# Attention and a mixture of adapters on one core: the stores of a tile, the queue of transposes and the order table

## The chip, the cores and the metric

The kernel runs on one core of a Trainium2 chip. The metric is the device time of one execution in microseconds. The kernel before took 182.09 us (median of three runs, 181.49 to 182.18).

The core's engines each work through their own list of instructions, in order: TensorE (PE; its weight loads are PEld), VectorE (DVE), ScalarE (ACT), GpSimd (POOL) and SyncE (SP). SP does nothing but issue transfers. Transfers run on 16 DMA engines, whichever engine issued them.

## The reference

```python
scores = scale * np.matmul(q, k.transpose(0, 1, 3, 2))     # 8 batches, 12 heads, 448 rows, 64 wide
attn = np.maximum(scores, 0.0) ** 2 / S
attn_out = np.matmul(attn, v)
x = attn_out.transpose(0, 2, 1, 3).reshape(3584, 768)
logits = x @ w_gate                                        # 8 experts
# the two best experts of a row, weighted by a softmax over the two
delta[row] += w[row, e] * (x[row] @ A[e]) @ B[e]           # A: 768x16, B: 16x768
return x + delta                                           # 3584 x 768, float32
```

The attention uses a squared ReLU in place of a softmax, so no row has to be normalised. The adapters are low-rank: 16 columns per expert, and the eight experts side by side make 128.

## The kernel before, in words

**Attention.** Twelve heads are four by four: three groups `q` of four heads, called quads, for each of the eight batches `b`. A quad goes through seven steps `j` of 64 key rows, each step with all 448 query rows, which makes 21 steps per batch and 174 steps `n` in all (the last 128 query columns of batch 7 are a part of their own, with several `j` in one step). The words of a step are `qk n` (scores, TensorE, into two PSUM banks), `relu n` (ACT or DVE, PSUM to SBUF in bf16), `sq n` (DVE, squares two or three steps at once) and `pv n` (TensorE, accumulates over the seven steps). `x m` copies the finished quad into `k.xt`, the transposed output of the attention (ACT or DVE). `tp` and `te` transpose the q and k of the next quad on TensorE and copy them out on DVE. The loads of q, k and v are cast to bf16 on the way and are issued from POOL, two transfers for each tensor of a quad (`load`, L185). Their words are `f` and a number: `f14` is k of quad 2, `f15` v of quad 0, `f16` q of quad 3, `f17` k of quad 3, `f22` the two instructions that make the selection matrix `sel`.

**Adapters.** The 3584 output rows are 28 tiles `t` of 128 rows, two blocks `j` of 64 rows each. For a group of three tiles `z` projects on all experts and the gate, the words `gmax` to `gzp` choose and weigh two experts, `zt` and `zT` transpose the weighted projection. Then for each tile and each half `h` of its 768 columns, `b 2t+h` multiplies with `B` (L714) and adds x by three matmuls with an identity (L705); `o 2t+h` copies the result from PSUM to the buffer `osb` (L743), and `st 2t` stores the tile (L760). For tiles 15 to 23 x doesn't come from matmuls: SP transposes `k.xt` back by DMA, six transposes for a group of three tiles (`turned`, words `xb`, L655), and `o` adds them on DVE (L734).

**The order.** The whole program is written in the order of the table `ORDER`: 1113 words, from which each engine gets its own list. `:A` or `:D` names the engine of a copy, `@` the first PSUM bank. A search made the table offline, with a cost for each word that stands in `build` as `op(engine, microseconds, ..., lat=...)`; these costs do nothing in the kernel. An engine waits where its next instruction waits, with all that stands behind it.

**Buffers.** `POOLS` gives the number of each: four of `osb`, eight of v, five each of q and k, three of `xb`. A buffer is free again when the last instruction that uses it is done; for `osb` that is when the store has landed. A tile that needs a buffer takes one whose store stands earlier in the table.

**Stores.** `st` (L752) walks the 128 rows of a tile in runs of 64, one transfer each. The output is seen as `out.rearrange("(b p j) f -> b j p f", b=8, j=7)`: a block `j` is 64 rows `p` that lie seven output rows apart, each 768 floats (3,072 bytes) long. The stores of tiles 24 and 26 are issued from ACT, those of the others from SP; tile 27 is stored in two halves of its columns, one from SP and one from ACT. The search gave a store 1.4 us of its queue and a landing 1.9 us later, and made each `xb` wait for the store of the tile six before its group (`xlag`).

Of the kernel before, what the change touches and what calls it, by code (L numbers as in the profile page):

```python
# [14 lines left out]
J = 7  # L15
# [14 lines left out]
PARTS = {b: ((0, S, 1),) for b in range(NB)}  # L30
PARTS.update({7: ((0, 320, 1), (320, 448, 4))})


C = dict(late=6, xi=(), om=(), merge_x=0, sqs=(2, 2, 3), xback=(15, 23), xblat=1.4, xbdur=1.35, bx=8, xlag=6, xh=2, apart=3, apcap=1, gl=(3, 1), tqlat=2.0)
GROUP = 2688
POOLS = dict(qT=5, a=11, zp=2, zT=3, osb=4, w=3, q=5, k=5, v=8, xb=3)
# [3 lines left out]
f4 f3 f1 f0 f2 f6 f5 f8 f7 f11 f9 f10 f84@0 f12 f88 f85@2 f90 f89 f13 f87@4 qk0@6 f91 qk1@0 qk2@2 relu0:D qk3@4  # L40
f14 relu1:A relu2:D relu3:A tp2@6 f17 qk4@0 relu4:A te2 qk5@4 qk6@2 sq2 relu5:A tp3@6 f16 f86@0 relu6:A te3 sq0
qk7@0 f15 qk8@4 qk9@6 relu7:A tp4@2 relu8:D relu9:A f18 qk10@0 te4 qk11@4 relu10:A qk12@6 sq4 tp5@2 relu11:A f19
qk13@0 relu12:A te5 tp6@4 f26 relu13:A sq9 qk14@2 qk15@6 tp7 relu14:A f23 sq7 pv0@0 pv1 pv2 relu15:A pv3 qk16@2
te6 pv4 pv5 relu16:A f20 pv6 qk17@6 x13:D pv7@4 relu17:A qk18@2 sq11 pv8 f22 pv9 x12:A qk19@6 relu18:A pv10
qk20@0 relu19:D f21 pv11 relu20:A pv12 pv13 qk21@2 x27:A sq16 qk22@6 f27 qk23@0 relu21:A aw1@5 sq14 relu22:A f33
relu23:A x26:D qk24@2 tp8@6 ae1 f25 relu24:A qk25@0 sq18 qk26@4 tp9 relu25:A f55 pv14@2 pv15 pv16 relu26:A pv17
te8 qk27@0 pv18 f31 pv19 relu27:A pv20 sq23 qk28@4 qk29@6 x41:A f28 qk30@0 relu28:A x40:D aw0@3 sq25 relu29:A
f29 relu30:A qk31@4 tp10@6 ae0 tp11 relu31:A f32 sq21 qk32@0 qk33@2 relu32:A te10 pv21@4 pv22 f30 relu33:A pv23
qk34@0 sq30 qk35@6 relu34:A qk36@2 f37 relu35:D relu36:A qk37@0 pv24 pv25 pv26 relu37:A sq32 qk38@2 f35 tp12@6
pv27 relu38:A tp13 qk39@0 x55:A te12 f43 qk40@2 x54:A z0@5 relu39:A sq35 qk41@6 f34 z1 relu40:A qk42@0 relu41:D  # L50
z2 relu42:A qk43@2 f38 gmax0 relu43:A tp14@6 sq28 qk44@0 tp15 relu44:A f42 qk45@2 gd0 gu0 te14 relu45:A qk46@0
gt0 relu46:A f50 sq39 qk47@6 pv28@2 pv29 pv30 gsg0 pv31 relu47:A qk48@0 f24 pv32 pv33 gw0 sq44 pv34 relu48:A f48
qk49@6 x69:A gzp0 tp18@0 relu49:A tp19 sq37 f36 pv35@4 zt0@3 zt1 zt2 x68:A qk50@6 te18 zT0:A pv36 f41 pv37
relu50:A qk51@2 pv38 sq46 pv39 relu51:A pv40 qk52@0 f47 qk53@6 pv41 relu52:A tp16@2 x82:D tp17 relu53:A te16
qk54@0 b2@4 relu54:A sq49 f44 qk55@6 o2:A qk56@2 qk57@0 relu55:A relu56:D b0@4 f49 x83:A relu57:D qk58@6 o0:A
qk59@2 relu58:A z3@5 z4 f39 sq51 relu59:A qk60@0 qk61@6 z5 sq56 relu60:A b4@4 f40 relu61:A gmax3 qk62@2 sq58
b1@0 relu62:A f46 gu3 gd3 o4:A qk63@6 gt3 sq42 qk64@2 gsg3 o1:A b3@1 f65 relu63:A gw3 b5@4 gzp3 relu64:A sq60
f51 zt3@0 zt4 zt5 o3:A pv42@6 pv43 o5:A qk65@2 st2 pv44 zT3:A pv45 sq53 qk66@4 relu65:A pv46 pv47 pv48 tp20@0
relu66:A st4 qk67@2 tp21 x96:D x97:A f53 te20 pv49@4 relu67:A pv50 qk68@6 st0 pv51 pv52 relu68:A pv53 sq63 f66
pv54 pv55 qk69@0 qk70@2 x110:A relu69:D qk71@6 f45 relu70:A b6@4 relu71:A x111:D qk72@0 o6:D tp22@2 relu72:A  # L60
sq65 qk73@6 tp23 pv56@4 pv57 relu73:A f74 qk74@0 te22 pv58 pv59 relu74:A pv60 qk75@6 f79 pv61 sq67 pv62 relu75:A
qk76@2 b8@0 relu76:A x124:D qk77@6 f64 x125:A sq70 tp24@2 relu77:A tp25 qk78@4 z6@1 te24 f59 relu78:A qk79@6 z7
relu79:A o8:D qk80@4 qk81@2 f52 sq72 z8 relu80:A b10@0 relu81:A gmax6 sq77 f54 qk82@6 tp26@4 o10:A tp27 qk83@2
relu82:A gd6 gu6 b7@0 te26 f56 relu83:A qk84@6 gt6 o7:D qk85@4 gsg6 relu84:A qk86@2 gw6 f70 sq74 b9@0 relu85:A
pv63@6 pv64 relu86:A gzp6 pv65 qk87@4 pv66 sq79 pv67 relu87:A pv68 pv69 zt6@1 zt7 x139:A x138:D zt8 qk88@2 o9:A
qk89@4 zT6:D qk90@6 relu88:A st8 relu89:D tp28@0 tp29 relu90:A qk91@2 f80 te28 pv70@4 pv71 relu91:A pv72 pv73
qk92@6 f60 sq84 pv74 pv75 relu92:A pv76 qk93@0 b14@2 x153:D x152:A f58 relu93:A sq81 qk94@6 tp30@4 o14:A tp31
pv77@0 relu94:A pv78 f77 qk95@2 te30 pv79 pv80 relu95:A pv81 qk96@6 pv82 f57 sq91 pv83 relu96:A qk97@4 b11@2
relu97:D x166:A f67 b12@3 x167:A o11:A sq93 qk98@6 o12:A st10 qk99@0 qk100@4 relu98:A relu99:D b13@2 relu100:A
z9@3 st6 sq88 qk101@6 o13:A tp32@0 qk102@4 relu101:A tp33 b15@2 st12 f62 sq86 relu102:A qk103@6 o15:A te32 f61  # L70
qk104@4 relu103:A z10 z11 sq100 relu104:A qk105@0 f69 pv84@6 pv85 pv86 relu105:A gmax9 qk106@4 pv87 sq95 f72
pv88 relu106:A pv89 pv90 qk107@0 x181:A qk108@4 f63 gd9 gu9 x180:A relu107:D b16@2 relu108:A gt9 qk109@6 o16:D
f81 pv91@0 gsg9 pv92 relu109:A gw9 pv93 sq105 qk110@4 pv94 pv95 relu110:A pv96 f78 qk111@6 gzp9 pv97 relu111:A
x195:D zt9@2 zt10 qk112@4 sq98 x194:A zt11 f75 b17@3 relu112:A zT9:D qk113@6 o17:A sq102 pv98@0 qk114@4
relu113:A pv99 st16 tp36@2 pv100 tp37 relu114:A pv101 qk115@6 te36 pv102 pv103 relu115:A st14 pv104 tp34@4 tp35
f83 sq109 qk116@2 x209:A qk117@6 x208:A b20@1 relu116:A f68 te34 b22@0 relu117:A f71 sq114 o20:A qk118@2 qk119@4
qk120@6 relu118:A b21@1 f73 sq112 o22:A b23@2 relu119:A o21:D z12@3 sq107 relu120:A st20 qk121@0 qk122@4
relu121:A z13 relu122:D z14 o23:A qk123@6 pv105@0 gmax12 pv106 relu123:A qk124@4 gd12 pv107 gu12 pv108 gt12
sq116 pv109 relu124:A pv110 pv111 qk125@6 f82 b18@2 gsg12 relu125:A gw12 x223:D x222:A qk126@4 f76 o18:D qk127@6
relu126:A b19@1 gzp12 sq121 relu127:A zt12@0 zt13 zt14 qk128@2 pv112@4 pv113 o19:D relu128:A qk129@6 pv114  # L80
zT12:D pv115 st18 pv116 relu129:A pv117 sq123 pv118 tp38@2 qk130@0 x236:A tp39 qk131@6 st22 relu130:A b24@4 te38
relu131:A tp42@0 sq119 tp43 x237:A qk132@2 b25@6 relu132:A te42 xb90 b28@7 o24:A o25:A sq128 xb93 qk133@2 o28:A
qk134@4 tp40@0 relu133:A sq126 pv119@6 tp41 pv120 relu134:A pv121 xb91 qk135@2 te40 pv122 pv123 relu135:A pv124
pv125 qk136@4 x251:D xb94 qk137@0 x250:A b29@2 sq130 relu136:A b26@3 st24 relu137:A sq135 o29:A qk138@6 qk139@4
o26:A qk140@0 xb92 z15@2 relu138:A relu139:D z16 z17 relu140:A qk141@6 st28 gmax15 pv126@4 pv127 relu141:A gd15
pv128 gu15 qk142@0 gt15 sq133 pv129 pv130 gsg15 pv131 relu142:A xb108 qk143@6 pv132 gw15 b27@3 gzp15 x264:A
x265:D relu143:A zt15@2 xb111 zt16 zt17 sq137 pv133@0 o27:A qk144@4 tp44@6 zT15:A pv134 tp45 relu144:A xb95
qk145@2 pv135 te44 pv136 relu145:A pv137 qk146@4 pv138 pv139 st26 sq140 relu146:A z18@6 b30@7 x279:A sq142 z19
x278:A xb109 qk147@2 qk148@4 qk149@0 o30 relu147:A z20 sq144 b32@7 relu148:A xb112 relu149:A b33@2 gmax18 xb110
qk150@4 o32 qk151@0 relu150:A b31@3 gu18 o33 relu151:A gd18 qk152@4 sq149 st32 b34@7 relu152:A gt18 o31 gsg18  # L90
qk153@0 qk154@4 gw18 o34 relu153:A b35@2 st30 gzp18 relu154:A qk155@0 o35 pv140@6 relu155:A pv141 sq151 qk156@4
xb113 pv142 pv143 relu156:A qk157@2 qk158@0 pv144 pv145 relu157:D relu158:A pv146 tp46@4 tp47 x293:A x292:D
qk159@0 qk160@2 relu159:A zt18@7 te46 zt19 xb126 zt20 z21@6 relu160:A z22 sq156 zT18:A qk161@0 qk162@4 qk163@2
relu161:A xb129 b40@7 sq147 relu162:A z23 sq158 relu163:A qk164@0 xb127 pv147@4 pv148 pv149 relu164:A pv150
qk165@2 o40 pv151 pv152 relu165:A pv153 sq154 qk166@0 xb130 b41@7 relu166:A gmax21 x307:A gu21 qk167@2 gd21
pv154@0 sq163 x306:A pv155 pv156 st34 relu167:A pv157 pv158 qk168@4 gt21 o41 pv159 gsg21 pv160 b36@2 gw21 x320:A
gzp21 xb128 x321:A b38@3 sq161 relu168:A zt21@7 zt22 sq165 zt23 qk169@0 st40 zT21:A pv161@4 pv162 pv163
# [47 lines left out]
def build(k=None, c=C):  # L145
# [104 lines left out]
    def aw_place(half, deps):  # L250
# [13 lines left out]
        def ev():  # L264
# [5 lines left out]


    order = [(b, u, q, range(j, min(j + PARTS[b][u][2], J))) for b in range(NB) for u in range(len(PARTS[b]))
             for q in range(QUADS) for j in range(0, J, PARTS[b][u][2])]
    NS = len(order)
    first_use, last_use = {}, {}
    head_of, heads = {}, {}
# [654 lines left out]
```

## Time and profile before

| | us |
|---|---|
| median of three runs | 182.09 |
| the profiled execution, its own time | 182.88 |
| its span, first to last instruction | 180.8 |
| PE busy | 165.2 (91%) |
| DVE busy | 163.6 (90%) |
| ACT busy | 156.4 (87%) |
| POOL busy | 89.9 (50%) |
| first store issued | 61.9 |
| last matmul begins | 175.4 |
| last store issued | 177.0 |

The busy times are those of the page's first part; a span holds idle time at both ends, about 7 us until the first step and 4.3 us after the last copy. Three engines are near 90% busy over the whole span, and all three are nearly without a gap between 24 and 160 us. "Busy" counts an instruction from its start to its modelled end; matmuls overlap, so PE's figure is an upper one. The share of a DMA queue is the time that its packets took, as a share of 16 engines' time; packets of one engine can overlap, so that slices over 1 occur.

### The profile page before, as it was taken

The numbers are of one execution on the slowest core, as the hardware profiler recorded it, in microseconds if no ns is written. First come the engines' busy times: TensorE is split into PE (matmuls) and PEld (weight loads), VectorE is DVE, ScalarE is ACT, GpSimd is POOL, SyncE is SP. The second block draws the span as 40 slices with busy tenths as digits, with TensorE's granted clock in tenths as the row PEclk, the third lists the DMA queues.
The fourth block names the chain that finished last, engine by engine and source line by source line (L and its number), as shares of the span: only waits on it lengthen the run. The fifth ranks groups of instructions, "written<-read, shape, count | busy, mean of one in ns | idle before, by whom it ended". The sixth has DMA issues, their size and how long they took to land.

```text
span 180.8 us, 7744 instructions
## 1 busy us (share of the span) xinstructions
PE 165.2 (91%) x3366; PEld 99.2 (55%) x3366; DVE 163.6 (90%) x254; ACT 156.4 (87%) x240; POOL 89.9 (50%) x155
## 2 busy tenths in 40 slices
PE   7777889788999999999999899999999999999990
PEld 2434466454555565655646475655666557676640
DVE  0799799999989999999999899999999999999740
ACT  3499899999999999999999999999999899992120
POOL 7998998979669377760877487340000000000000
PEclk9997899999999999999999999999999999999999
DMA  5999999999999999996599999997376579467875
GB/s 94 127 175 180 156 142 179 182 184 164 214 142 146 186 237 194 176 178 141 68 143 287 224 181 259 224 170 202 68 126 144 131 175 110 101 149 176 227 215 172
DMA packets 34450, 30.50 MB, mean 169 GB/s; under 512 B 11952, under 2 KB 30896, under 8 KB 34416
## 3 DMA queue, kind: packets, MB, share of 16 engines
q0 software_dynamic: 22000, 17.03, 64.9%
q1 hardware_dynamic: 11792, 11.90, 26.5%
q10 hardware_dynamic: 624, 1.08, 2.2%
q8 instruction: 26, 0.43, 1.0%
q14 instruction: 8, 0.07, 0.1%
HBM read 33.84 MB, written 11.01 MB: 248 GB/s over the span
## 4 chain that ended last, share of the span: by engine, by line
PE 51%; ACT 27%; POOL 7%; DMA 6%; issue 4%; DVE 3%; ACTq 0%; DVEq 0%; POOLq 0%
ACT a L468 24%; PE ps L714 18%; PE ps L449 11%; PE ps L516 10%; DMA q<-in_q_dram 6%; PE ps L560 4%; PE ps L310 3%; PE ps L705 3%; POOL q L185 3%; POOL k L185 3%; PE ps L622 2%; ACT osb L743 2%; DVE a L485 2%; ACT xt L544 1%; POOL k_rest L216 1%
## 5 line engine op out<-in xcount | busy, mean ns | idle before, releaser
L468 ACT ACTIVATE a<-ps 128x896 bf16<-128x896 f32 (+3 forms) x158 | 132.6, 952 | 3.7 <-PE ps L449 3.1
L485 DVE TENSOR_TENSOR a<-a 128x1792 bf16<-128x1792 bf16 (+3 forms) x75 | 89.0, 1200 | 0.0
L449 PE MATMUL ps<-qT 64*64 64x448 bf16 (+2 forms) x756 | 58.1, 342 | 3.9 <-ACT a L468 2.4
L714 PE MATMUL ps<-B,zT 128*128 128x384 f32 x112 | 47.5, 515 | 0.0
L516 PE MATMUL ps<-a,v 64*64 64x448 bf16 (+2 forms) x756 | 45.3, 335 | 1.6 <-DVE a L485 1.3
L449 PEld LDWEIGHTS <-qT 64*64 64x64 bf16 x756 | 25.1, 105 | 31.8 <-issue 23.2
L185 POOL DMA_DIRECT2D k<-in_k_dram x46 | 27.9, 629 | 18.2 <-PE ps L310 7.3
L185 POOL DMA_DIRECT2D v<-in_v_dram x48 | 29.0, 629 | 6.2 <-PE ps L449 1.8
L185 POOL DMA_DIRECT2D q<-in_q_dram x48 | 29.4, 651 | 4.9 <-DMA v<-in_v_dram 2.7
L516 PEld LDWEIGHTS <-v 64*64 64x64 bf16 x756 | 22.7, 108 | 9.0 <-issue 4.1
L324 DVE COPY qT<-ps 128x1792 bf16<-128x1792 bf16 x21 | 22.8, 1085 | 0.2
L544 ACT CAST xt<-ps 128x448 bf16<-128x448 f32 (+2 forms) x37 | 19.0, 554 | 2.9 <-PE ps L516 2.7
L743 ACT COPY osb<-ps 128x384 f32<-128x384 f32 x26 | 13.1, 523 | 7.1 <-PE ps L714 4.1
L714 PEld LDWEIGHTS ps<-B,zT 128*128 128x128 f32 x112 | 17.3, 190 | 3.3 <-issue 0.3
L470 DVE TENSOR_SCALAR a<-ps 128x896 bf16<-128x896 f32 (+1 forms) x16 | 16.9, 1067 | 0.5 <-PE ps L449 0.5
L310 PEld LDWEIGHTS <-q 64*64 64x64 bf16 x672 | 10.4, 111 | 6.3 <-issue 2.5
L560 PEld LDWEIGHTS <-xt 128*128 128x128 bf16 x168 | 10.5, 98 | 5.8 <-issue 4.7
L560 PE MATMUL ps<-awg,xt 128*128 128x136 bf16 x168 | 13.5, 223 | 0.0
L705 PEld LDWEIGHTS <-xt 128*128 128x128 bf16 x114 | 8.0, 98 | 9.9 <-issue 8.1
L310 PE MATMUL ps<-identb,q 64*64 64x64 bf16 x672 | 10.8, 196 | 2.5 <-DMA q<-in_q_dram 1.3
L705 PE MATMUL ps<-identb,xt 128*128 128x128 bf16 x114 | 12.7, 220 | 0.2
L544 DVE CAST xt<-ps 128x448 bf16<-128x448 f32 (+2 forms) x17 | 9.6, 571 | 2.2 <-PE ps L516 2.2
(47 smaller groups left out, 97.5 us busy)
## 6 DMA issues: line engine op xcount, KB each, us to landing
out_dram<-osb SPq DMA_DIRECT2D x50, 192.0 KB, 3.9
q<-in_q_dram POOLq DMA_DIRECT2D x48, 112.0 KB, 4.8
v<-in_v_dram POOLq DMA_DIRECT2D x48, 112.0 KB, 5.0
k<-in_k_dram POOLq DMA_DIRECT2D x46, 112.0 KB, 5.1
out_dram<-osb ACTq DMA_DIRECT2D x4, 192.0 KB, 2.9
B<-in_moe_B_dram POOLq DMA_DIRECT2D x1, 384.0 KB, 8.0
xb<-xt SPq DMA_TRANSPOSE x18, 3.1
a_raw<-in_moe_A_dram POOLq DMA_DIRECT2D x1, 192.0 KB, 5.2
```

The lines of the kernel that those rows point to most:

```text
L185: nc.gpsimd.dma_start(out=t[g * PH : g * PH + PH], in_=k.qkv[w][b, g, :, 2 * q : 2 * q + 2, :])
L310: nc.tensor.transpose(k.ps_b[sl * PH : sl * PH + PH, o.banks[g], (w * J + j) * PH : (w * J + j) * PH + PH], source(w, j)[r, sl], k.identb[ ...
L324: nc.vector.tensor_copy(t.rearrange("p g w x -> p g (w x)"), k.ps_b[:, m.banks[0] : m.banks[0] + 2, : 2 * S])
L449: nc.tensor.matmul(out=bank(o, sl)[g * PH : g * PH + PH, at : at + w], lhsT=t[r, g, 1, j * PH : j * PH + PH], rhs=t[r, g, 0, x0:x1], start ...
L468: nc.scalar.activation(out, flat(qk_ops[n], w), ACTF.Relu, scale=k.relu_scale)
L470: nc.vector.tensor_scalar(out, flat(qk_ops[n], w), k.relu_scale, 0.0, op0=ALU.mult, op1=ALU.max)
L485: nc.vector.tensor_mul(a, a, a)
L516: nc.tensor.matmul(out=bank(head, g)[sl * PH : sl * PH + PH, :w], lhsT=vn[r, sl, j * PH : j * PH + PH], rhs=T["a", g0][r, x + sl * width(n ...
L544: evac(w, lambda cp, g=g: cp(k.xt[:, g * QUADS + q, b * S + x0 : b * S + x1], bank(src, g)[:, :w]), deps=[pv_ops[n]], free=[(src, g)], key ...
L560: nc.tensor.matmul(out=bank(zops[0])[:, t * ZW : t * ZW + ZW], lhsT=k.xt[:, do, 128 * tiles[t] : 128 * tiles[t] + 128], rhs=k.awg[:, do, : ...
L705: nc.tensor.matmul(out=out(h)[:, x * 128 : x * 128 + 128], lhsT=k.xt[:, 3 * h + x, c0 : c0 + 128], rhs=k.identb, start=(x == 0), stop=Fals ...
L714: nc.tensor.matmul(out=o, lhsT=T["zT", g0][:, zi], rhs=rhs, start=xb is not None, stop=True, skip_group_check=True,)
```

## The change

1. A tile whose two blocks lie in one batch is stored by one transfer instead of two: 128 rows of `osb`, against `out[b, j0 : j0 + 2, :, :]`. Tiles 3, 10, 17 and 24 lie across two batches and keep two transfers of 64 rows. The two halves of tile 27 become one transfer each.
2. The order table is another one. Nearly all words have the same engines as before; `zT9` and `zT24` move from DVE to ACT and `zT27` from ACT to DVE.
3. `xb` has two buffers instead of three, and an `xb` has no wait for a store of another tile in the search's model.
4. The costs that the search uses are others: 0.75 us of the queue for a store of one transfer, a landing after 2.3 us, 1.45 us for a transpose and 1.55 us plus 0.15 per tile until it lands.
5. New options (`sqp`, `om2`, `fl`, `gf`, `ai`, `tg`, and a fourth entry in `PARTS`) are at values that give the former program.

```diff
-PARTS = {b: ((0, S, 1),) for b in range(NB)}
-C = dict(late=6, ..., sqs=(2, 2, 3), xback=(15, 23), xblat=1.4, xbdur=1.35, bx=8, xlag=6, xh=2, ...)
+PARTS = {b: ((0, S, 1, range(QUADS)),) for b in range(NB)}
+C = dict(late=6, ..., sqp=((999, (2, 2, 3)),), om2=(), fl=(), gf=(), ai=4, tg=((15, 3), (18, 3), (21, 3)), sp=(), xbdur=1.45, bx=8, xh=2, ...)
-POOLS = dict(qT=5, a=11, zp=2, zT=3, osb=4, w=3, q=5, k=5, v=8, xb=3)
+POOLS = dict(qT=5, a=11, zp=2, zT=3, osb=4, w=3, q=5, k=5, v=8, xb=2)
...
 ORDER
-f14 relu1:A relu2:D relu3:A tp2@6 f17 qk4@0 relu4:A te2 qk5@4 qk6@2 sq2 relu5:A tp3@6 f16 f86@0 relu6:A te3 sq0
-qk7@0 f15 qk8@4 qk9@6 relu7:A tp4@2 relu8:D relu9:A f18 qk10@0 te4 qk11@4 relu10:A qk12@6 sq4 tp5@2 relu11:A f19
-qk13@0 relu12:A te5 tp6@4 f26 relu13:A sq9 qk14@2 qk15@6 tp7 relu14:A f23 sq7 pv0@0 pv1 pv2 relu15:A pv3 qk16@2
+relu1:A qk3@4 relu2:D relu3:A tp2@6 f14 qk4@0 te2 relu4:A qk5@2 sq2 tp3@4 f16 relu5:A qk6@6 te3 relu6:A f22 sq0
+qk7@0 qk8@2 tp4@4 relu7:A qk9@6 relu8:D relu9:A f17 qk10@0 te4 qk11@2 relu10:A qk12@6 f18 sq7 tp5@4 relu11:A
+pv0@0 pv1 te5 f23 relu12:A qk13@2 sq4 pv2 f86@4 relu13:A qk14@6 pv3 f20 qk15@4 relu14:A sq9 tp6@2 pv4 relu15:A
+f28 qk16@6 sq11 tp7 pv5 relu16:A qk17@4 pv6 f19 relu17:A te6 pv7@6 pv8 pv9 x13:A f25 qk18@4 sq14 x12:A pv10
...
+st22 relu126:A gw12 x222:D qk127@6 st2 o18:D relu127:A qk128@2 qk129@0 gzp12 xb90 b19@5 relu128:A sq121 zt12@4
...
-b54@1 o49:A st49 b55@7 o54:D st54 o55:D st55
+zt27@6 b52@7 o51:D zT27:D o50:D b53@3 o52:A st50 b54@2 o53:A st53 b55@3 o54:D st54 o55:A st55
...
-                ts[do] = op(("SP",), c["xbdur"], lambda do=do: turn(do), kind="turn", deps=list(dict.fromkeys(deps)) + [st_of[t0 - c["xlag"]]],
+                ts[do] = op(("SP",), c["xbdur"], lambda do=do: turn(do), kind="turn", deps=list(dict.fromkeys(deps)),
...
+        (b0, j0), (b1, j1) = (divmod((c0 + r) // PH, J) for r in (0, PH))
 
         def st(e, c1=0, c2=2 * W):
-            r = 0
-            while r < 128:
-                b, x = divmod(c0 + r, S)
-                j, p = divmod(x, PH)
-                m = min(PH - p, 128 - r)
-                if b >= c["bx"]:
-                    j = TURNED[j]
-                {"SP": nc.sync, "ACT": nc.scalar, "POOL": nc.gpsimd}[e].dma_start(
-                    out=k.out[b, j, p : p + m, c1:c2], in_=T["osb", tl][r : r + m, c1:c2])
-                r += m
+            dma = {"SP": nc.sync, "ACT": nc.scalar}[e].dma_start
+            if b0 == b1:
+                dma(out=k.out[b0, j0 : j0 + 2, :, c1:c2], in_=T["osb", tl][:, c1:c2])
+                return
+            for i, (b, j) in enumerate(((b0, j0), (b1, j1))):
+                dma(out=k.out[b, j, :, c1:c2], in_=T["osb", tl][i * PH : i * PH + PH, c1:c2])
```

In the new table the store of tile 1 (`st2`) stands behind that of tile 11 (`st22`), and k of quad 18 (`f65`) is loaded ahead of k of quad 5. POOL now makes `sel` ahead of the load of k of quad 3, and loads v of quad 0 ahead of k of quad 2.

## The prediction

> **What bounds the kernel now.** I read the page first, then the busy times by stretches, then the DMA answers of three stretches.
>
> ```profile
> span 180.8 us, 7744 instructions
> PE 165.2 (91%) x3366; PEld 99.2 (55%) x3366; DVE 163.6 (90%) x254; ACT 156.4 (87%) x240; POOL 89.9 (50%) x155
> ...
> out_dram<-osb SPq DMA_DIRECT2D x50, 192.0 KB, 3.9
> ```
>
> Three engines share the limit; no store delays any of them. The stretches show it stage by stage:
>
> ```profile
> 60.00:80.00 20.00, 19.48 (x449) 11.91 (x447) 19.90 (x30) 20.00 (x30) 13.30 (x23) 1.00 1.14 196
> 140.00:164.00 24.00, 23.99 (x413) 15.15 (x412) 23.80 (x46) 21.52 (x38) 0.00 (x0) 1.00 0.64 130
> 170.20:176.50 6.30, 5.69 (x33) 3.11 (x30) 3.25 (x7) 1.25 (x5) 0.00 (x0) 1.00 0.83 228
> ```
>
> Columns: length, then PE, PEld, DVE, ACT, POOL busy, clock, DMA share, GB/s. Up to 164 us a changed order has little idle time to win; after it TensorE alone works, on the last `b`. Among the waits of ACT and DVE none names a store or an `xb`, so SP's queue, retimed by this change, costs nothing today.
>
> Now one tile's store, whose two transfers fall in a stretch without loads (DMA answer for 83.1 to 86.4 us):
>
> ```profile
> DMA packets 162, 0.39 MB, mean 119 GB/s; under 512 B 33, under 2 KB 34, under 8 KB 162
> ...
> q1 hardware_dynamic: 160, 0.39, 46.3%
> ...
> out_dram<-osb SPq DMA_DIRECT2D x2, 192.0 KB, 2.6
> ```
>
> 160 packets are 128 rows and 32 four-byte packets, 16 for each transfer: each ran on all 16 DMA engines, four rows apiece. Their time is 0.463 x 16 x 3.3 us = 24.4 us, or 191 ns a row. In the packet records of the whole trace a 3,072-byte row takes 119 ns at the least, 134 in the median, 179 in the mean. Landing 2.6 us after issue is four rows (0.5 us) and 2.1 us of fixed cost.
>
> ```profile
> q0 software_dynamic: 8886, 7.08, 83.4%
> q1 hardware_dynamic: 1600, 3.93, 21.9%
> ```
>
> That is 62 to 120 us: the loads take 0.834 x 58 = 48 us of packet time on every DMA engine after the first store is issued at 61.9 us; after 120 us there are none.
>
> **The change, part by part.**
>
> *One transfer for 128 rows.* It removes an issue per tile (median 588 ns of SP, which waits anyway: worth nothing inside). What it adds is a new shape. In every transfer of the trace the outermost count is 64 or 128, on both sides; here it is 128 in `osb` but 2 (the blocks `j0`, `j0+1`) in the output. No row shows over how many DMA engines such a pair is dealt. Bounds: 16 engines, like every row, 8 rows each, 2.1 + 8 x 0.134 = 3.2 us until landing and nothing lost; or as many as the smaller outermost count, two, 64 rows each. On two engines a tile holds both for 64 x 119 ns = 7.6 us (nearly empty fabric) to 64 x 191 ns = 12.2 us, and lands 2.1 us later. I take two: all the rows fit a dealing along the outermost count of both sides, and none shows that an inner count (the 64 of `p`) is dealt out. Per row I take 130 ns, nearest the median, as two engines crowd each other less than sixteen: 8.3 us a tile.
>
> [...]
>
> Tiles come every (176.5 - 61.9) / 28 = 4.1 us, so two engines at 8.3 us can't follow. With four `osb` buffers (three, once tile 1 keeps its own until `st2`, behind `st22`), the third or fourth tile in arrears makes `o` wait for a landing: on ACT or DVE, with `relu` and `sq` queued behind, TensorE next for want of PSUM banks. Then the pair of DMA engines sets the pace from 62 us to the end:
>
> - 23 whole tiles x 8.3 = 191 us (28 less the four across batches and tile 27);
> - tile 27's two halves, 64 rows of 1,536 bytes each on either engine, half price: 2 x 4.2 = 8 us;
> - tiles 3, 10, 17, 24 at 16 engines: 4 x 8 rows x 0.13 = 4 us;
> - loads: 48 us of packet time, of which 16 us put as hindrance. Ends 0 (all beside stores; the DMA share of 1.14 above shows that packets overlap) and 48;
> - after the last row 2.1 us, and 1.0 from the last landing to the end, as before (the store issued at 177.0 lands at 179.8; span 180.8).
>
> 62 + 191 + 8 + 4 + 16 + 3 = 284 us of span. The profiled execution's own time is 2.1 above its span and 0.8 above the median, so 285 us.
>
> *The order table*, with every buffer on time. Engine totals hardly move: same counts of `relu`, `x`, `o` on ACT and DVE; `zT` takes 2 x 0.55 from DVE and returns 0.3. Start: ACT and DVE now idle 0.9 and 1.3 us near 19 us, since `tp6` waits for q of quad 3 (landed 16.0) and `pv0` to `pv3` precede `qk16`. In the new table k of quad 3 is issued after `sel` (two instructions of 0.83 us), at 13 to 14.3, and lands near 18.7; but only `tp7` and `qk17` stand behind it, so `relu17` starts near 19.3 instead of 20.4: -1.2, bounds -1.7 and +1. Middle: from `relu99` to the end I count 75 us of PE rows before and 77 after (0.19 for a `qk` or `pv` of 448 columns, 0.87 for a `b`, 0.35 for a `z`; two more `b` still to do): +1.8, less 1.1 us of ACT work done earlier. The load of v of quad 14 now waits for `pv90` and is due about 5 us later at `pv98`: 0 to +2, taken +0.5. End: the last issue is one instead of two: -0.5 of issue, +0.1 landing. Sum -0.8. Under the stores' pace all this is covered: it costs nothing unless the stores keep up.
>
> *`xb` with two buffers, no bond to stores.* Group 21's first transpose needs the buffer of group 15, free at `o35`; SP has time before `o42`. Nothing with 16 engines. With two, the transposes stand in SP's own queue behind whole stores (rival 1). *New options* at old values: nothing.
>
> **The rivals.**
>
> 1. *Two engines, but not kept busy.* `o32` needs `xb92`, which stands on SP behind the store of tile 12, one more than `o32`'s own buffer waits for: 8.3 + 2 us there. Ten or so waits for a buffer each leave the pair idle while a tile's second half is computed, some 2.5 us. 285 + 35 = 320. For it: three free buffers, and tiles held 10 to 25 `relu` long. Against: three buffers are up to two stores of work in hand.
> 2. *The rows are dealt over 16 engines*: not slower, 182.1 - 0.8 = 181.3. For it: 16 small packets at every transfer so far. It decides from four engines up, where a tile holds them 32 x 0.13 = 4.2 us, the 4.1 us of its production. Within it new stalls of the table (v of quad 14, `o16` seven `relu` after the store that frees its buffer, while landings reached 7.7 us) may bring 183 to 185.
> 3. *One engine*: 62 + 23 x 16.6 + 17 + 19 = 480.
>
> **How the numbers follow.** Forecast 0.56, rival 1 0.27, rival 2 0.14 (of it 0.04 faster, 0.05 within, 0.05 slower by more than 0.5%, about what a measurement of this kernel can tell), rival 3 0.03. So slower 0.91, same 0.05, faster 0.04. The range: low, 62 + 23 x 7.6 + 8 + 4 + 0 + 3 = 252, plus 1.3 for the time around it, less 8 as packets of one engine overlap (4% off the 7.6, a share like the 1.14 above): 245. High: rival 1 with all 48 us of the loads, 320 + 32 = 352: 350. It leaves out rivals 2 and 3 and a few tails: 0.2.
>
> **What would show it.** Right: two small packets a store instead of 16, so far fewer q1 packets; landings near 10 us and more at the median; waits of ACT or DVE in `o` (L743, L734) for the store's transfer; in the last slices a DMA share near 2/16 = 0.13 and some 50 GB/s; PE's share of the span near 60%. Wrong: landings of 3 to 4 us and no such waits, and then rival 2's sums apply: `relu17` near 19.3 us, TensorE without a gap from 100 us on. Wrong in size: the row price on a lone pair is not 130 ns, or the loads hinder more.

## The result and the profile after

The changed kernel takes 313.16 us (median of six runs, 309.66 to 314.33). The kernel before, on the same chip, takes 182.09 us (181.49 to 182.99). The ratio is 1.714, with a 95% interval of 1.704 to 1.724. Ratios below, too, are of undisturbed runs (only two of the six for the run with two transfers), and the profiles of three experiments (two transfers, swapped rows, seven buffers) are of executions at a lower clock, so events are read from them, not their whole spans.

The profiled execution took 313.49 us, with a span of 311.7. From its page come the span, the engines, three rows of the 40 slices (PE busy, the granted clock of PE, the share of the DMA engines, in tenths), two queues and the issues of the store; the last line is the clock's row of the page before:

```profile
span 311.7 us, 7701 instructions
PE 186.3 (60%) x3366; PEld 107.2 (34%) x3366; DVE 163.0 (52%) x253; ACT 159.8 (51%) x241; POOL 90.1 (29%) x155
...
PE   7889979996089791880978390099466850242000
...
PEclk9599999999679997595599776579975995555555
DMA  7999999977688795383332149912994111311110
...
q1 hardware_dynamic: 11102, 11.90, 22.4%
q10 hardware_dynamic: 564, 1.08, 1.1%
...
out_dram<-osb SPq DMA_DIRECT2D x22, 384.0 KB
```

```profile
PEclk9997899999999999999999999999999999999999
```

DVE and ACT are busy for as long as before (163.0 and 159.8 us against 163.6 and 156.4); they have only been stretched over 130 us more. PE's 186.3 against 165.2 is no extra work: the instruction count is the same 3,366, and the granted clock, which is 0.9 or more in 38 of the 40 slices before, falls to 0.5 to 0.7 in slices where PE stands idle and in those after them (one slice at the start, ahead of any store, is at 0.5 too).

The queue line tells over how many engines the stores went. Before, every transfer of a store left 16 packets of four bytes beside its rows (q1's 1,424 such packets are 53 x 16 for the stores and one load, and 18 x 32 for the transposes). SyncE issued 25 whole tiles and one half tile as pairs: 26 x 2 x 16 = 832 such packets. If a merged store leaves two, SyncE now leaves 22 x 2, 3 x 32 for the tiles across two batches, and 2 for the half tile, 142 in all. The difference would be 690. q1 fell from 11,792 to 11,102, which is 690. q10 (ScalarE's) fell by 60 = 64 + 32 - 36 in the same manner: tile 24 keeps 32, tile 26 has 2 in place of 32, the half 2 in place of 32.

The waits, the costliest first (engine, tile and line, what it waited for: us in total, times, longest):

```profile
ACT osb L770 <- DMA out_dram<-osb: 64.0, 8, 15.8
DVE osb L770 <- DMA out_dram<-osb: 34.1, 3, 16.2
...
DVE osb L761 <- DMA out_dram<-osb: 20.9, 5, 6.9
...
DVE osb L761 <- DMA xb<-xt: 15.2, 1, 15.2
```

L770 and L761 are L743 and L734 of before: the eviction into `osb`. Before, no wait of ACT or DVE named a store; now 119 us do (64.0 + 34.1 + 20.9). The first two merged stores on the chain that ended last took 24.2 and 13.6 us until they landed (start, us, what):

```profile
61.25 24.19 DMA out_dram<-osb
...
93.49 13.64 DMA out_dram<-osb
```

Two stretches near the end (length, PE, PEld, DVE, ACT, POOL busy, clock, DMA share, GB/s):

```profile
280.00:300.00 20.00, 1.86 (x5) 0.71 (x4) 0.56 (x1) 1.15 (x3) 0.00 (x0) 0.50 0.13 53
300.00:311.70 11.70, 0.00 (x0) 0.00 (x0) 0.00 (x0) 0.00 (x0) 0.00 (x0) 0.50 0.11 41
```

Almost nothing but stores is left, and they move at 53 GB/s with a share of 0.13 = 2/16. The DMA answer for 250 to 262 us has the price of a row:

```profile
DMA packets 204, 0.62 MB, mean 52 GB/s; under 512 B 2, under 2 KB 2, under 8 KB 204
...
q1 hardware_dynamic: 204, 0.62, 12.8%
```

202 rows took 0.128 x 16 x 12 us = 24.6 us, or 122 ns each. In the packet records two tiles that ran alone (192.6 to 200.1 and 201.5 to 209.1) took 7.6 us for 64 rows on each engine, 118 ns a row or 26 GB/s per engine.

Over the whole trace, row packets of stores are in flight for 219.9 us between 62.2 and 309.8, with 27.7 us of gaps: 62.2 + 219.9 + 27.7 + 1.9 to the end = 311.7.

### The profile page after: what moved, and what is told of

It reads as the page before. It is cut to its first block, busy times and chain, and to the rows that moved or that the text cites. A ratio compares the mean times of both kernels' runs of the same rounds, so it can differ in the third digit from the quotient of the medians.

```text
span 311.7 us, 7701 instructions
## 1 busy us (share of the span) xinstructions
PE 186.3 (60%) x3366; PEld 107.2 (34%) x3366; DVE 163.0 (52%) x253; ACT 159.8 (51%) x241; POOL 90.1 (29%) x155
## 3 DMA queue, kind: packets, MB, share of 16 engines
q1 hardware_dynamic: 11102, 11.90, 22.4%
## 4 chain that ended last, share of the span: by engine, by line
DMA 42%; PE 19%; DVE 14%; issue 7%; ACT 5%; SPq 3%; POOL 3%; ACTq 0%; DVEq 0%; POOLq 0%
DMA out_dram<-osb 38%; DVE a L488 7%; PE ps L734 5%; PE ps L452 5%; ACT a L471 4%; PE ps L519 4%; DVE qT L327 3%; SPq L674 3%; DMA xb<-xt 3%; DMA k<-in_k_dram 2%; DVE a L473 1%; PE ps L725 1%; POOL q L185 1%; PE ps L313 1%; PE ps L579 1%
## 5 line engine op out<-in xcount | busy, mean ns | idle before, releaser
L452 PE MATMUL ps<-qT 64*64 64x448 bf16 (+2 forms) x756 | 67.2, 367 | 53.9 <-ACT a L471 22.5
L734 PE MATMUL ps<-B,zT 128*128 128x384 f32 x112 | 56.1, 598 | 4.7 <-DVE osb L761 4.7
L452 PEld LDWEIGHTS <-qT 64*64 64x64 bf16 x756 | 28.0, 112 | 86.5 <-issue 76.7
L519 PE MATMUL ps<-a,v 64*64 64x448 bf16 (+2 forms) x756 | 52.0, 355 | 6.0 <-issue 4.8
L770 ACT COPY osb<-ps 128x384 f32<-128x384 f32 x26 | 13.2, 515 | 76.1 <-DMA out_dram<-osb 64.0
L185 POOL DMA_DIRECT2D k<-in_k_dram x46 | 27.8, 618 | 15.1 <-PE ps L313 5.5
L761 DVE TENSOR_TENSOR osb<-ps,xb 128x384 f32<-128x384 f32 x18 | 9.9, 553 | 39.1 <-DMA out_dram<-osb 20.9
L519 PEld LDWEIGHTS <-v 64*64 64x64 bf16 x756 | 25.1, 113 | 15.0 <-issue 10.8
L770 DVE COPY osb<-ps 128x384 f32<-128x384 f32 x12 | 6.6, 550 | 36.4 <-DMA out_dram<-osb 34.1
L734 PEld LDWEIGHTS ps<-B,zT 128*128 128x128 f32 x112 | 20.5, 222 | 9.2 <-DVE osb L761 5.2
L725 PE MATMUL ps<-identb,xt 128*128 128x128 bf16 x114 | 14.3, 242 | 12.1 <-DVE osb L770 7.7
L725 PEld LDWEIGHTS <-xt 128*128 128x128 bf16 x114 | 8.9, 108 | 25.8 <-issue 24.8
L579 PEld LDWEIGHTS <-xt 128*128 128x128 bf16 x168 | 11.0, 100 | 7.7 <-issue 5.3
```

The source lines that it names most:

```text
L185: nc.gpsimd.dma_start(out=t[g * PH : g * PH + PH], in_=k.qkv[w][b, g, :, 2 * q : 2 * q + 2, :])
L452: nc.tensor.matmul(out=bank(o, sl)[g * PH : g * PH + PH, at : at + w], lhsT=t[r, g, 1, j * PH : j * PH + PH], rhs=t[r, g, 0, x0:x1], start ...
L519: nc.tensor.matmul(out=bank(head, g)[sl * PH : sl * PH + PH, :w], lhsT=vn[r, sl, j * PH : j * PH + PH], rhs=T["a", g0][r, x + sl * width(n ...
L579: nc.tensor.matmul(out=bank(zops[0])[:, t * ZW : t * ZW + ZW], lhsT=k.xt[:, do, 128 * tiles[t] : 128 * tiles[t] + 128], rhs=k.awg[:, do, : ...
L725: nc.tensor.matmul(out=out(h)[:, x * 128 : x * 128 + 128], lhsT=k.xt[:, 3 * h + x, c0 : c0 + 128], rhs=k.identb, start=(x == 0), stop=Fals ...
L734: nc.tensor.matmul(out=o, lhsT=T["zT", g0][:, zi], rhs=rhs, start=xb is not None, stop=True, skip_group_check=True,)
```

## The experiments

### Two transfers again, in the new order (e1_two)

```diff
-            if b0 == b1:
-                dma(out=k.out[b0, j0 : j0 + 2, :, c1:c2], in_=T["osb", tl][:, c1:c2])
-                return
```

> The kernel after, its order and buffers kept, with every store again as two transfers of 64 rows; nothing of the computation is changed. Theory (the merged store's two DMA engines are the whole loss, and the order is worth -0.8 us): about 181.3, in bounds of 180 to 185; the small packets come back (q1 near 11,792, q10 near 624) and the wait of the copies and adds of osb for stores is gone. Rival (the new order or its buffers are the loss, xb cut to two among them): about 300.

Measured: ratio 1.020 [1.011, 1.028] to the kernel before, some 185.3 us. q1 is back at 11,792. So the order, the `xb` buffers and all else that changed with the store account for some 3.5 us of the 131 (2.0 to 5.1 by the interval); the merged store is the rest. The expected 181.3 was missed, in part by a wait that the prediction had priced at nothing. SyncE's line of time, from the profile of this run (start, length with what lies between, line, what, count):

```profile
120.77 10.81 SPq L674 DMA_TRANSPOSE xb<-xt  x5
131.67 1.18 SPq L784 DMA_DIRECT2D out_dram<-osb  x2
132.89 3.23 SPq L674 DMA_TRANSPOSE xb<-xt  x2
136.22 1.17 SPq L784 DMA_DIRECT2D out_dram<-osb  x2
137.44 6.03 SPq L674 DMA_TRANSPOSE xb<-xt  x4
```

There is hardly a pause in it: SyncE's own waits between 117 and 146 us add up to 6.5 us, none longer than 1.7. `xb92`, the third block that `o30` (tile 15) adds, is the second of the last four. `x250`, the last copy into `xt` that it reads, ended at 130.4; `xb92` was issued at 138.8 and landed at 142.5. The waits of the run say what that cost:

```profile
DVE osb L761 <- DMA xb<-xt: 4.2, 1, 4.2
```

The table was searched with one short issue a store (0.55 us in the trace of the swapped run below); here each store takes 1.2 us of the queue. So this run carries a burden that the changed kernel doesn't have.

### The same, five stores taken off SyncE (e8_pool)

```diff
-STORES = {24: 'ACT', 26: 'ACT'}
+STORES = {1: 'POOL', 9: 'POOL', 10: 'POOL', 11: 'POOL', 12: 'POOL', 24: 'ACT', 26: 'ACT'}
...
```

> The run with after's order and two transfers a store (fast runs 184.1 to 186.4), with the stores of tiles 1, 9, 10, 11 and 12 issued by GpSimd in place of SyncE; nothing of the computation is changed. In that run SyncE's queue worked without a pause from 116.95 to 143.5 us, the turn for output block 2 of tile 15 stood there until 138.8 though its data was there at 130.4, and the add of tile 15 waited 4.2 us for it. Theory (SyncE's queue, loaded by the second transfers, is what makes that run slower than before): five pairs of issues (5 x 1.2 = 6 us) leave the queue, the wait is gone, 180.5 to 183. Rival (the loss lies elsewhere in the order): 184 to 187 as without it.

Measured: 184.56 us median, ratio 1.011 [1.007, 1.016], about 183.9. `xb92` is issued at 134.3, 4.5 us earlier, and the wait of L761 for `xb` is gone from the list. So the wait was SyncE's backlog, as expected, but its removal brought only some 1.5 us, if anything (the intervals overlap). By the ratio the time lies between the two expectations, by its median in the rival's: the rest, about 2 us, is elsewhere in this run and wasn't traced to one place.

### The old order with the merged store (e2_before_one)

```diff
...
+            if b0 == b1:
+                dma(out=k.out[b0, j0 : j0 + 2, :, c1:c2], in_=T["osb", tl][:, c1:c2])
+                return
...
```

> The kernel before, its order and buffers kept, with one transfer of 128 rows where both of a tile's blocks lie in one batch; nothing of the computation is changed. Theory: the pair of engines needs 7.6 us a tile alone and some 9 to 11 beside loads, so about 300 to 320, as the kernel after. Rival (the order is the loss): about 182.

Measured: 308.96 us, ratio 1.701 [1.689, 1.712]. One edit of the store in the kernel before gives 127 of the 131 us, with the same queue line as the changed kernel:

```profile
span 306.2 us, 7704 instructions
...
q1 hardware_dynamic: 11102, 11.90, 25.1%
```

### One transfer, but its rows in another order (e3_swapped, e6_before_swapped)

The store stays one transfer of 128 rows. Row and block change places, so the outermost count in the output is 64. The columns of `xt` are written in that order, which takes two copies where there was one.

```diff
-                dma(out=k.out[b0, j0 : j0 + 2, :, c1:c2], in_=T["osb", tl][:, c1:c2])
+                dma(out=k.out[b0, j0 : j0 + 2, :, c1:c2].rearrange("j p f -> p j f"), in_=T["osb", tl][:, c1:c2])
...
+            cp(t[:, y : y + m].rearrange("f (t p j) -> f t j p", j=2, p=PH),
+               bank(src, g)[:, y : y + m].rearrange("f (t p j) -> f t j p", j=2, p=PH))
```

> The kernel after with one transfer of 128 rows as before, but its rows in the order (row, block) in place of (block, row), so that the outermost count on the DRAM side is 64 and not 2. For that the copies into xt write the columns of two blocks in turns, in two instructions in place of one (54 more copies, some 0.15 to 0.25 us each on ScalarE and VectorE, both busy 87% before: up to 6 us of the span). The computation is the same. Theory (the outermost count sets how many engines carry a transfer): 16 engines, 181 to 190, and 16 small packets a store again. Rival (a single transfer of 128 rows is slow by itself, through its one issue or its one completion): 290 or more.

Measured (in the changed kernel): ratio 1.016 [1.009, 1.022], some 184.6 us. 128 us of the loss are gone, with the same 384 KB in the same single issue. The page's queue line of this run:

```profile
q1 hardware_dynamic: 11424, 11.90, 19.4%
```

That is 368 below before = 22 x 16 + 16: 16 small packets for each merged store and for SyncE's half of tile 27. The single transfer isn't slow; the two in front of its count is.

The same edit in the kernel before:

> The kernel before, its order and buffers kept, with one transfer of 128 rows in the order (row, block) where both blocks lie in one batch, and the two-instruction copies into xt that this needs; the computation is the same. It is to the run with swapped rows (after's order, fast runs 183.3 to 185.6) what before's order is to after's. Theory of the prediction (after's order is worth -0.8 us): 184 to 187, a little above that run. Rival (after's order is by itself 1 to 3 us slower): 181 to 183. In both, 16 small packets a store.

Measured: 184.52 us, ratio 1.016 [1.012, 1.020]. Its page lists the landing of the 384 KB transfer over 16 engines:

```profile
out_dram<-osb SPq DMA_DIRECT2D x22, 384.0 KB, 3.9
```

Both orders come out at the same 1.016: with one short issue a store they differ by less than these runs can tell (about 0.8%). The 2.9 us above before go with the second copies, which keep ACT busy for 159.7 us in place of 156.4 and DVE for 164.7 in place of 163.6; that they alone make them was not tried apart.

### Eight buffers (e4_osb8)

```diff
-POOLS = dict(qT=5, a=11, zp=2, zT=3, osb=4, w=3, q=5, k=5, v=8, xb=2)
+POOLS = dict(qT=5, a=11, zp=2, zT=3, osb=8, w=3, q=5, k=5, v=8, xb=2)
```

> The kernel after with eight buffers of osb in place of four; nothing of the computation is changed. Theory (the pair of engines is the pace and the buffers only pass it on): the pair's 220 us of busy time stay, the 28 us of gaps shrink; 62 + 220 + 2 = 284 at the least, 285 to 312. Rival (waits for buffers are the cost by themselves): below 250.

Measured: 306.97 us, ratio 1.690 [1.679, 1.701]. Twice the buffers buy 6 us of 131 by the medians, 4.5 by the ratios. Store rows are in flight for 218.2 us (219.9 with four buffers) from 62.2 to 302.7, with 22.3 us of gaps (27.7 with four). The wait that leads the list is now another:

```profile
DVE osb L761 <- DMA xb<-xt: 34.4, 1, 34.4
```

In the changed kernel a transpose that SyncE began to issue at 192.9, while a tile's rows, the only store, ran from 192.6 to 200.1, landed at 201.4: 8.5 us, against 3.1 in the median before. In the packet records no packet of a transpose begins between 196.3 and 200.0. So that one came behind a whole store; that with eight buffers more stores stand before them is inferred from the longer wait. The pair of engines is the pace (218.2 us against 219.9); here the buffers only changed who waits.

### Merging only some stores (e7_quarter, e9_half)

The kernel before, with one transfer in 6 of the 23 whole tiles, or, with `tl % 2 == 0`, in 12.

```diff
...
+            if b0 == b1 and tl % 4 == 1:
...
```

> The kernel before with the merged store (outermost count 2) in six tiles alone: 1, 5, 9, 13, 21 and 25; nothing of the computation is changed. Theory (the loss is the throughput of one pair of engines, and comes once the pair is always busy): 6 x 9.5 = 57 us of work for the pair in the 118 us from 62 to 180, so most of it is hidden, 182 to 187. Rival (each merged store costs its own time on the path, 131 us over 23 tiles = 5.7 us each): 182 + 34 = 216.

> The kernel before with the merged store (outermost count 2) in twelve tiles alone: 0, 2, 4, 6, 8, 12, 14, 16, 18, 20, 22 and 26; nothing of the computation is changed. Theory (throughput of one pair): 12 x 9.5 = 114 us of work in the 118 us from 62 to 180, at the brink: 184 to 205, and any excess shows in the second half. Rival (each store costs 5.7 us on the path): 182 + 68 = 250.

Measured: six merged stores 208.81 us, ratio 1.148 [1.141, 1.155], +27 us or 4.5 each; twelve 232.56 us, 1.278 [1.270, 1.286], +51 us or 4.2 each. With 23 it was 127 (old order), 5.5 each. My theory, that stores cost nothing until the pair is always busy, failed here: with six stores the pair has room (rows of any store are in flight for 97 us of the 144 from 62 to 206), and yet 27 us are lost. The rival's number (216) was nearer, though not its even spread. Against the trace of before, instructions fall behind in steps: `relu108` is on time, `relu116` is 8.2 us late, `relu144` 10, `relu172` 12, `o55` 21, and the end 26.

The steps are not all of one kind. In the run with six, the two large ones are evictions that wait. At 102 to 110 DVE waits 6.5 us for something that the profile doesn't name (the next experiment shows that it is a buffer); near the end it waits for a store to land:

```profile
DVE osb L743 <- DMA out_dram<-osb: 8.2, 1, 8.2
```

Other steps are late loads and transposes. These are spread over 16 engines (before, the 147 loads issued from POOL left 147 x 16 small packets and the 18 transposes 18 x 32), so a part of each stands behind the 64 rows on two of them; the records don't name the engine of a packet, so this is inferred from how late they land. From the chain of the run with twelve (start, us, what):

```profile
83.61 13.31 DMA q<-in_q_dram
```

That load was issued at 83.6 and came in 13.3 us later; the median of that page is 5.1 (before, 4.8 for loads of q). PE had nothing to do and `relu92` was 14.8 us late. In the run with six, the transpose on the chain was no better off (7.7 us to landing; before, the median is 3.1):

```profile
153.02 1.19 SPq L655
154.26 3.09 SPq L655
157.39 7.73 DMA xb<-xt
```

### Six merged stores with seven buffers (e11_quarter_osb7)

```diff
-POOLS = dict(qT=5, a=11, zp=2, zT=3, osb=4, w=3, q=5, k=5, v=8, xb=3)
+POOLS = dict(qT=5, a=11, zp=2, zT=3, osb=7, w=3, q=5, k=5, v=8, xb=3)
```

> The run with six merged stores (208.8), with seven buffers of osb in place of four; nothing of the computation is changed. In that run the instructions fall behind those of before in steps: 8 us at 102 to 110 and 7 us at 184 to 197, both where an eviction into osb waits for a store to land, about 6 us at 145, 168 and 175, and 5 us between the last eviction and the end. Theory (a merged store lands late, and where tiles are finished in a bunch four buffers don't bridge that): the two buffer waits go, the rest stays, 182 + 11 = 193, in bounds of 188 to 198. Rival (what the pair delays is something else, loads or the engines of all later stores, so that more buffers only move the wait): 203 to 209.

Measured: 204.87 us, ratio 1.115 [1.107, 1.123] or some 202.4. Closer to the rival. The step at 102 to 110 is gone (`relu112` is 0.6 us late in place of 6.4), so that one was a wait for a buffer. The one at the end only moved: the last eviction isn't held up, but 16 us of stores follow it (4.3 before). These are the two stretches of that end:

```profile
176.00:188.00 12.00, 10.85 (x84) 6.39 (x83) 8.42 (x28) 2.40 (x9) 0.00 (x0) 1.00 0.71 188
188.00:204.00 16.00, 0.00 (x0) 0.00 (x0) 0.16 (x1) 0.00 (x0) 0.00 (x0) 0.64 0.31 81
```

Tiles are finished in a bunch there. Two of them are merged, 2 x 64 rows on each of the pair's engines; six whole ones and the halves of tile 27 are split, 6 x 8 rows of 3,072 and 16 of 1,536 bytes on every engine. At 118 ns a row, and 72 for the short ones (next experiment), that is 15.1 + 5.7 + 1.2 = 22.0 us for the pair, and the records show 26.3 (176.1 to 202.4).

And a step of 2.0 us between `relu140` and `relu144` had grown to 6.9; in it PE waited for nothing that the profile names:

```profile
139.48 0.52 PE L560 MATMUL ps<-awg,xt 128*128 128x136 bf16 x3 [4.32 <-issue]
```

What it may be is told in the last section.

### The two halves of tile 27 alone (e10_last)

```diff
...
+            if tl == NT - 1:
+                dma(out=k.out[b0, j0 : j0 + 2, :, c1:c2], in_=T["osb", tl][:, c1:c2])
+                return
...
```

> The kernel before with the two halves of tile 27 alone as merged stores (128 rows of 1,536 bytes each, outermost count 2), one on SyncE's queue, one on ScalarE's; nothing of the computation is changed. Nothing hides these: they are the last transfers. In before their packets run from 177.4 to 179.3 us. Theory (both queues' merged stores share the same two engines, some 59 to 65 ns a row on each): 2 x 64 rows in 7.6 to 8.3 us, so 177.4 + 8 and 1.5 for the end: span 187, time 188, +5.5 to +6.5. Rival (each queue has its own pair): 3.8 to 4.2 us, time 184, +2 to +2.5. Rival (16 engines): one issue less on each queue, 181.2 to 181.8.

Measured: 189.66 us, ratio 1.046 [1.041, 1.051], +8.1 us, where nothing else differs. The stretch that holds both halves, and the DMA answer for 174 to 190 us:

```profile
182.00:185.00 3.00, 0.00 (x0) 0.00 (x0) 0.00 (x0) 0.00 (x0) 0.00 (x0) 0.50 0.13 50
```

```profile
q10 hardware_dynamic: 294, 0.59, 14.2%
q1 hardware_dynamic: 290, 0.59, 13.6%
```

SyncE's half runs from 178.1 to 184.9, ScalarE's from 180.7 to 187.4, and while both run the share is 0.13: two engines, not four. Both queues' merged stores go to the same pair. 128 rows of 1,536 bytes on each engine take 9.3 us, 72 ns a row: half the bytes cost more than half, so the 59 to 65 of the expectation was too low, and with it the 188.

## Why the prediction was right, and where it wasn't

**The step that decides: two engines.** Right. The packet counts have it to the packet (690 of 690), and swapping row and block in the very same transfer gives 16 engines and 184.6 us. So the runs show two engines with an outermost count of 2 in the output, and 16 with 64; no run has a store with a count between. That 2 would give two was my inference, from transfers that all ran on 16.

**The pair's work.** The sum had 191 + 8 + 4 + 16 = 219 us; 219.9 were measured. The sum is better than its terms, which is luck. A tile takes 7.6 us and not 8.3, so 23 take 175 and not 191 (the 130 ns a row was 8 to 12 too high, the lower bound of 119 was the value). Tile 27's halves, alone, take 9.3 and not 8. Taking away these and the 4 of the tiles across batches leaves, as a remainder, 32 for the hindrance by loads and transposes; I had put 16, between 0 and 48.

**"The pair sets the pace from 62 us to the end."** This is the step that failed, and it is the whole difference between 284 and 311.7 us of span: 27.7 us of gaps, which I had at nothing in the forecast and at 35 in rival 1. Three gaps are long: 84.9 to 93.7, 106.8 to 111.7 and 175.0 to 183.3; six short ones add up to 5.7 us. In the first two an eviction on ACT got its buffer when a store landed (at 85.5 and 107.2), and the next store was issued only at 92.3 and 108.9. That is rival 1's wait for a buffer, in fewer and longer pieces than its ten of 2.5 us. The third is SyncE's queue. The store of tile 9 was ready when `o19` ended at 160.6, but stood in the table behind five transposes, which took SyncE until 182.1 (one of them, begun at 167.0, took 10.3 us to be issued), though what they read had been copied by 163.3:

```profile
156.13 25.89 SPq L674 DMA_TRANSPOSE xb<-xt  x5
182.13 0.52 SPq L784 DMA_DIRECT2D out_dram<-osb  x1
```

So rival 1's mechanism was there beside the forecast's, and its queue worked both ways: stores also wait behind transposes. The transpose that held DVE for 15.2 us (until 201.4) came while the pair had stores for all but some 2 us, so it made hardly any of the gaps. The range to 350 came from rival 1 and held it.

**Who waits.** I named `o`, on ACT and DVE, and PE next: right, 119 us of waits. I did not see that loads and transposes would come late as well (13.3 and 7.7 us to landing, where the medians before are 4.8 and 3.1) and, as it seems, instructions too, and so took a pair with room to cost nothing; six stores with +27 us show otherwise. For the full change that made no difference, for a smaller one it would have made the forecast wrong.

**The order, -0.8.** The terms as written add up to -0.4 (-1.2 + 1.8 - 1.1 + 0.5 - 0.5 + 0.1), which would make rival 2's time 181.7; the forecast doesn't use it. A gain was not confirmed either. With single stores on 16 engines both orders measure alike; with two transfers a store the new one is 1.1 to 2.0% slower. `relu17` starts at 19.8 us in the changed kernel (20.4 before; I said 19.3), but at 20.4 in the run with two transfers. The start proves nothing either: `relu60` comes 1.8 us earlier in the changed kernel and 1.3 in the run with two transfers, but also 0.6, 1.0 and 1.3 earlier in three executions of the old order whose edits do nothing up to there, and `relu17` starts between 19.5 and 20.9 in executions of the old order. "SP's queue costs nothing" holds for the old order alone: in the new one, with two issues a store, it ran from 117 to 143 us with no wait over 1.7 us, and a transpose that DVE needed came late.

**Rival 2** (181.3, sixteen engines) is what the swapped run comes nearest to, at 184.6 with its second copies; that it would decide from four engines on was not tried. **Rival 3** (480) is out. None of the runs beats the kernel before.

## What to carry to other kernels

Before two transfers are joined, look at the outermost count of the joined pattern on both sides, not at its rows or bytes: a 2 in front put 384 KB on two of sixteen engines, and it could be moved inwards because the rows were free to be in another order (here at the price of second copies, 1.6% over the kernel before). Read it afterwards from the small packets in the queue line and from a DMA share that stands still at a small fraction, here 2/16. A few transfers on few engines are no small matter: buffers come back late (waits of 6.5 and 8.2 us with six such stores), and what is spread over all engines seems to wait for its part that stands behind them (13.3 us for a load, median 4.8 before), so the loss starts long before the few engines are always busy (4 to 5 us for each such store here, on average and in uneven steps).

## What the runs showed of the hardware that I had not expected

**PE's own instructions seem to wait for the pair.** Queue q8 moves 26 packets of 16,384 bytes in a run, all through it; before, none takes more than 2.1 us. In the changed kernel one started at 166.0 and took 10.19 us. The DMA answer for 165 to 177 us has it (0.053 x 16 x 12 us = 10.2), and PE's line of time shows a wait with no other releaser, which ends 1.5 us after that packet:

```profile
q1 hardware_dynamic: 556, 0.60, 14.2%
q8 instruction: 1, 0.02, 5.3%
```

```profile
177.75 0.58 PE L519 MATMUL ps<-a,v 64*64 64x448 bf16 x1 [4.84 <-issue]
```

The same is in the two runs with six merged stores: a packet of 8.48 us from 129.4 and PE's wait until 139.48, a packet of 5.24 us from 136.0 and PE's wait until 142.9, at the same matmul of L560 in both, and each time PE goes on 1.6 to 1.7 us after the packet's end. Packets of over 4 us occur only in the six runs with merged whole stores (ten; 2.3 us at most in the others), and so do PE's waits of over 1.2 us without a named releaser (seven). Five of the seven end 1.5 to 1.7 us after a packet of q8, two of these after one of usual length; the longest, 10.8 us in the run with eight buffers, ends 8.7 us after the packet before it and stays unexplained. If this reading is right, it cost PE 4.8 us here. That the packet holds PE's instructions and lies on one of the pair's engines is inferred from its length, its time and the name of its queue's kind, `instruction`; the trace names neither the engine that it feeds nor the one that it lies on, and no run took it apart.

**Two queues are no more engines.** SyncE's and ScalarE's merged stores of tile 27 shared one pair (0.13 = 2/16 with both running, from 182 to 185 us), so I expect no more engines from moving half of the stores to the other queue; that was not run.
